# An SSM and MLP gradient kernel: ten staging rows and moved parameter turns in the front, four seed columns and four doublings in the Y tables

## Chip, cores and metric

The kernel runs on one core of one Trainium2 chip. The metric is the device time of one execution in microseconds (us). The core has a matrix engine (PE, TensorE), a vector engine (DVE, VectorE), a scalar engine (ACT, ScalarE), a general engine (POOL, GpSimd) and a queue engine (SP, SyncE). DMAs are issued on the queues of SP, ACT and POOL.

## What is computed

The reference mixes two branches by a gate and returns the result and all gradients of it. In its core (dt, A, B, C are the state model's parameters for 448 channels with 256 complex states each, L = 2048 positions; the MLP's hidden width is 1792):

```python
g = sigmoid((u * gate_w).sum(-1))
P = exp(dt * A * l)                             # 448 x 256 x 2048
K = einsum("dn,dnl,dn->dl", C, P, dt * B).real  # 448 x 2048
a = irfft(rfft(pad(u)) * rfft(pad(K)))[:L] + u * Dskip
h = relu(u @ w1 + b1) ** 2
out = g * a + (1 - g) * (h @ w2 + b2)
# and the gradients of out (weighted with grad_out) in u, A, B, C, log_dt, Dskip, w1, b1, w2, b2, gate_w
```

## The kernel before

The work falls into a front, a loop over 14 chunks of states and a tail. The order of the instructions on each engine is made by a scheduler when the kernel is built; a statement may be placed behind another one with `tc.issue_after`. All transfers of SP and ACT go over a few shared semaphores, and an issue waits until the transfer before it on its semaphore has landed.

**The front** (about 0 to 236 us). u and grad_out are loaded in eight and four pieces on SP's and ACT's queues (L401, L411). `fwd1` (L219 to L241) is the first stage of the forward Fourier transform. It goes over eight blocks; a block makes four products (L229), evacuates them from PSUM into one staging row (L206, L207, L216) of 128 x 4 x 448, and stores its two halves to a tensor in memory, `gd`: the first half on POOL's queue, the second on SP's (L238). It runs on u first, with four rows in the buffer F17; the first five blocks are evacuated by ACT alone, the others by ACT and DVE in turn. On SP's queue the six parameters A, B, C (real, imaginary) are turned by DMA transposes (L420 to L423), and the constants M2, MI, Etw and sel are loaded (L424 to L426). These ten issues stand ahead of the second-half stores. The gate is computed (L456 to L463), DA = grad_out * g (L465), and `fwd1` runs on DA with six rows in R32 (L494). Then follow the parameter mathematics on DVE, with an exponential and a sine on ACT (L526 to L551), and `transposed` (L471 to L486), which turns u on PE, copies each block out of PSUM with ACT and DVE in turn (L483) into a ring of three slots, and spills a slot to memory on POOL's queue (L485). A second call does the same for DB = grad_out * (1 - g).

`powers(gr)` (L617 to L647) makes the records of a group of four chunks (two in the last group): starting from the transition factor of each state it squares ten times (ACT's Square L643, DVE L644 and L645), and ACT copies each power into the record (L640). A record has 1920 columns: four X seeds, the X powers, two Y seed columns (a one, set by POOL at L615, and one power) and five Y powers. The record of a group is stored on ACT's queue (L647). Groups alternate between a record buffer in F17 and one in R32. Between the groups run the spectra (`spectrum`, L657) and the first inverse transforms (`inv1p`, L280) of the products; their results are loaded back, summed (L713) and stored (dk).

**The chunk loop** (L965 to L1006, about 184 to 625 us). For each chunk DVE builds an X table (L794, L773 to L777) and a Y table: `build_y` copies the seed columns (L825) and doubles the table five times; each doubling (`double`) is three DVE instructions (L784, L785, L787), the last doubling in two halves. `expand_y` on ACT (L812, L814) widens the powers for the doublings, one chunk ahead. PE multiplies the tables into the convolution kernel (L844), turns them (L870, L882) and makes the chunk's gradient (L913 on PE, L917 on ACT, L933 on DVE, L942 on PE). Between these the scheduler places the MLP's products on PE: the hidden layer (L584, L587), the output (L1021), turns of the weights (L1045, L1056) and the first gradient products (L1084, L1087, with ACT L1089 and DVE L1096).

**The tail** (from about 651 us). The convolution kernel is loaded, the transform `fwd1` runs on it (L229 with the tensor `gd` number 2), and it stands in PE's order behind all of the output products L1021. The output, the weight gradients (L1158 to L1195), the parameter gradients and the last stores follow.

## Time and profile before

| | |
|---|---|
| median of 7 runs | 943.05 us (934.66 to 947.1) |
| the profiled execution | 944.72 us |
| its span in the profile | 942.5 us |
| its granted TensorE clock, mean | 0.833 of full speed |
| PE, DVE, ACT, POOL busy | 705.3, 670.9, 579.3, 191.8 us |
| u landed | 13.70 us |
| seed copies of the 14 chunks (L794) begin | 184.16, 214.30, 259.20, 291.22, 318.98, 346.68, 374.44, 402.17, 429.91, 460.02, 490.66, 526.87, 559.64, 591.48 us |
| bytes moved by DMA | 184.96 MB |

The profile is of one execution; its time is 2.2 us longer than the span, which runs from the first to the last instruction that the profiler shows. Busy time of an engine leaves out its waits and its DMA issues. A line such as "L216" is a line of the kernel's source; where a helper holds the instruction, several places of the kernel share the line, and the tile's name tells them apart (F is the buffer F17, R is R32, S is S25). In the lists of waits the name behind the arrow is what came last before the engine went on. A chain of waits follows what ended last back to what released it.

### The profile page before, as it was taken

The page shows a single profiled execution, that of the slowest core. Times are in us where ns is not written, and L with a number is a line of the kernel's source. Part 1 is how long each engine was busy: PE and PEld are TensorE (multiplying, and loading weights), DVE is VectorE, ACT ScalarE, POOL GpSimd, SP SyncE. Part 2 cuts the span into 40 slices and gives each one's busy share as a digit, 9 for nine tenths or more (in the row PEclk, how much of TensorE's full clock was granted, in tenths as well). Part 3 has the DMA queues.
Part 4 walks back from the last instruction along what each step waited for, and adds up shares of the span by engine and source line. Part 5 has one row for each costly group of instructions (what it writes and reads, how often), then busy time and mean ns, then how long its engine had stood idle before and what let it go on. Part 6 is the DMA issues. An engine that isn't in the chain of part 4 may idle for free.

```text
span 942.5 us, 18829 instructions
## 1 busy us (share of the span) xinstructions
PE 705.3 (75%) x7553; PEld 337.1 (36%) x7585; DVE 670.9 (71%) x1152; ACT 579.3 (61%) x927; POOL 191.8 (20%) x327
## 2 busy tenths in 40 slices
PE   3345675636878898788987898789958888959896
PEld 1122222214344443334443443444323334524343
DVE  4387985787389999999886899864219954159820
ACT  3346757725997879778686766564526644536543
POOL 2141000113202122121202311223201021343221
PEclk9686565668869999989966997999979778978799
DMA  9986486797536766446742964659997997589862
GB/s 188 254 254 242 161 308 254 277 319 232 119 82 126 156 137 121 117 102 144 179 104 77 246 160 125 124 144 282 331 377 241 245 281 234 180 211 288 205 149 73
DMA packets 170814, 184.96 MB, mean 196 GB/s; under 512 B 100467, under 2 KB 146968, under 8 KB 169800
## 3 DMA queue, kind: packets, MB, share of 16 engines
q1 hardware_dynamic: 121462, 84.74, 37.7%
q0 software_dynamic: 19904, 59.15, 19.6%
q10 hardware_dynamic: 29362, 39.88, 13.0%
q8 instruction: 59, 0.97, 0.4%
q14 instruction: 27, 0.22, 0.1%
HBM read 88.22 MB, written 73.13 MB: 171 GB/s over the span
## 4 chain that ended last, share of the span: by engine, by line
DVE 31%; DMA 18%; PE 18%; issue 14%; ACT 12%; POOL 4%; SPq 2%; ACTq 1%; POOLq 0%; DVEq 0%
DVE P L933 4%; DVE F L785 4%; PE psF L1169 3%; PE psN L1021 3%; DMA S<-rT_d 3%; DVE K L787 2%; DVE K L784 2%; DVE X L773 2%; DVE Y L787 2%; SPq L422 2%; DVE F L774 2%; DVE Y L784 2%; DMA hd<-st 2%; DVE X L777 1%; DMA D<-hd 1%
## 5 line engine op out<-in xcount | busy, mean ns | idle before, releaser
L933 DVE TENSOR_TENSOR P<-R 128x2048 bf16<-128x2048 bf16 x42 | 49.5, 1218 | 23.9 <-ACT R L917 21.1
L1169 PEld LDWEIGHTS <-S 128*128 128x128 bf16 x448 | 43.6, 104 | 59.9 <-issue 15.1
L917 ACT CAST R<-psF 128x1024 bf16<-128x1024 f32 x56 | 57.4, 1024 | 11.8 <-PE psF L913 11.7
L1021 PE MATMUL psN<-D,S 128*128 128x448 bf16 x208 | 52.5, 385 | 4.8 <-ACT S L591 4.8
L1169 PE MATMUL psF<-U,S 128*128 128x448 bf16 x224 | 51.7, 381 | 2.1 <-ACT S L1164 2.0
L913 PE MATMUL psF<-R,S 64*32 64x256 bf16 (+1 forms) x1344 | 37.9, 295 | 9.7 <-DMA R<-Y 5.2
L584 PE MATMUL psN<-S,U 128*128 128x512 bf16 x119 | 37.3, 419 | 10.2 <-ACT F L589 4.9
L1084 PE MATMUL psN<-S,U 128*128 128x512 bf16 x113 | 37.1, 441 | 7.5 <-ACT D L1089 5.5
L207 DVE CAST K<-psN 128x448 bf16<-128x448 f32 x36 | 21.6, 619 | 27.1 <-PE psN L255 26.9
L773 DVE TENSOR_TENSOR X<-X,F 128x512 bf16<-128x512 bf16 (+1 forms) x70 | 37.4, 535 | 4.6 <-ACT F L807 2.6
L784 DVE TENSOR_TENSOR K<-K,F 128x2048 bf16<-128x2048 bf16 (+3 forms) x42 | 36.4, 866 | 4.5 <-ACT F L812 2.9
L1097 POOL DMA_DIRECT2D dhT_d<-D x28 | 20.2, 721 | 90.9 <-DVE D L1096 90.7
L785 DVE TENSOR_TENSOR F<-K,F 128x2048 bf16<-128x2048 bf16 (+3 forms) x42 | 35.9, 855 | 3.1 <-ACT F L814 3.1
L784 DVE TENSOR_TENSOR Y<-Y,F 128x2048 bf16<-128x2048 bf16 (+3 forms) x42 | 36.3, 864 | 1.6
L774 DVE TENSOR_TENSOR F<-X,F 128x512 bf16<-128x512 bf16 (+1 forms) x70 | 36.9, 528 | 0.6
L787 DVE TENSOR_TENSOR K<-K,F 128x2048 bf16<-128x2048 bf16 (+3 forms) x42 | 36.3, 865 | 1.3
L787 DVE TENSOR_TENSOR Y<-Y,F 128x2048 bf16<-128x2048 bf16 (+3 forms) x42 | 36.3, 864 | 1.3
L1364 DVE SCALAR_TENSOR_TENSOR F<-psN,Y 128x448 bf16<-128x448 f32 x16 | 9.9, 616 | 36.9 <-PE psN L329 36.9
L785 DVE TENSOR_TENSOR F<-Y,F 128x2048 bf16<-128x2048 bf16 (+3 forms) x42 | 35.9, 854 | 0.3 <-ACT F L814 0.3
L1021 PE MATMUL psN<-S,D 128*128 128x448 bf16 x168 | 35.7, 361 | 0.0
L883 ACT COPY M<-psX 128x1024 bf16<-128x1024 bf16 x26 | 26.6, 1022 | 14.1 <-PE psX L882 14.1
L913 PEld LDWEIGHTS <-S 64*16 64x16 bf16 (+1 forms) x1792 | 22.4, 90 | 33.4 <-issue 28.5
(385 smaller groups left out, 1930.0 us busy)
## 6 DMA issues: line engine op xcount, KB each, us to landing
sp<-K ACTq DMA_DIRECT2D x8, 896.0 KB, 4.8
hd<-st ACTq DMA_DIRECT2D x16, 448.0 KB, 4.4
dhT_d<-D POOLq DMA_DIRECT2D x28, 256.0 KB, 5.3
R<-sp SPq DMA_DIRECT2D x8, 896.0 KB, 21.4
S<-rT_d POOLq DMA_DIRECT2D x14, 512.0 KB, 5.2
R<-hd SPq DMA_DIRECT2D x16, 448.0 KB, 7.2
rec_d<-F ACTq DMA_DIRECT2D x2, 1920.0 KB, 9.1
Y<-gd SPq DMA_DIRECT2D x4, 896.0 KB, 5.1
```

The lines of the kernel that those rows point to most:

```text
L584: T_.matmul(ps[:], lhsT=w1w[:, dt, j * P:j * P + P], rhs=ub[:, dt], start=(dt == 0), stop=False, skip_group_check=True)
L773: V.tensor_tensor(out=hi4, in0=lo, in1=bcast_dims(pr, [0, (None, n), 1]), op=ALU.mult)
L774: V.tensor_tensor(out=Vv.rearrange("p (x a r) -> p x a r", x=2 * W2, r=2), in0=lo, in1=bcast_dims(pi, [0, (None, n), 1]), op=ALU.mult)
L784: V.tensor_tensor(out=hi, in0=lo, in1=bcast_dims(pr, [0, (None, n // 2), 1]), op=ALU.mult)
L785: V.tensor_tensor(out=Vv.rearrange("p (x a q) -> p x a q", x=rows, q=2), in0=lo, in1=bcast_dims(pi, [0, (None, n // 2), 1]), op=ALU.mult)
L787: return V.tensor_tensor(out=T4[:, :, :, n:2 * n], in0=T4[:, :, :, n:2 * n], in1=V4, op=ALU.add)
L913: T_.matmul(psz[32 * ii:32 * ii + m, t, 256 * s:256 * s + 256], lhsT=DKc[64 * t:64 * t + 64, s, g, 2 * ii:2 * ii + 1 + par].rearrange("p i ...
L917: S.copy(zb[:, :, :, gg].rearrange("p s t n -> p t s n"), psz[:].rearrange("p t (s n) -> p t s n", s=2))
L933: lastp = V.tensor_tensor(out=pr.rearrange("p s t g n -> p s t (g n)"), in0=zv, in1=(xb if r == 0 else rev_dim(xb, 2)), op=ALU.mult)
L1021: lastm = T_.matmul(ps[:, 0:D], lhsT=hblk[j][:, P * tt:P * tt + P], rhs=ws[:, j, :], start=(w == 1 and j == 0), stop=(j == FT - 1))
L1084: T_.matmul(ps[:], lhsT=w2Tw[:, jp, dt, j % 2], rhs=dblk[:, dt], start=(dt == 0), stop=False, skip_group_check=True)
L1169: lastm = T_.matmul(ps[:, 0:width], lhsT=hh[:, t, :], rhs=(DB2[:, t, :] if w == 0 else U[:, t, 0:D + 1]), start=(t == 0), stop=(t == LT - 1))
```

## The change

- **Staging rows.** Both calls of `fwd1` take their rows from one list of ten (four in F17, six in R32). u takes F0 to F3 and R0 to R3, DA goes on with R4, R5, F0 to F3, R0, R1. DA's second-half stores are issued on ACT's queue.
- **Turns and constants.** The six parameter turns stay on SP's queue and are placed behind u's last second-half store. M2, MI, Etw and sel are loaded from ACT's queue; in the order of the built program they stand ahead of ACT's first evacuation.
- **transposed(u).** All eight copies are ACT's. The call for DB alternates as before.
- **Records.** A record has 2048 columns: four Y seed columns and four Y powers. The columns are one, the powers after two and after three squarings, and their product, which POOL makes with six tensor_tensor instructions a group (four products into a scratch behind DB in D16, a difference and a sum). The store of the record is issued on POOL's queue. Scratch buffers of the odd groups lie elsewhere.
- **Y tables.** The seed copy has four columns a row (128x512), and four doublings follow instead of five: the smallest, whose DVE instructions were 128x256, is gone. `expand_y` widens four levels (L812 on 128x1024, L814 on 128x512). A chunk's Y record load is 256 KB, not 224.
- **Tail.** A small row moves into the tile of the last Y record; the other line there is cut to the width in use.

```diff
 GC = 2
 W2 = 2 * CC
 NLEV = 11
-RS = 1920
+RS = 2048
 NA = 16
 AOFF = [0, 1, 2, 3, 256, 258, 512, 768, 1024, 1280, 1536, 1792, 2048]
 VA = len(AOFF)
...
         self.st_i = 0
         self.st_more = []
         self.q2 = tc.nc.gpsimd
+        self.q3 = tc.nc.sync
         self.pair_i = 0
         self.pairs3 = True
         self.act_only = False
...
                 j0base = 32 * hh + q * 4
                 for g2 in range(2):
                     dst = bass.AP(tensor=gd, offset=(j0base + 16 * g2) * 64 * D, ap=[[D, 64], [64 * D, 4], [1, D]])
-                    d = (self.q2 if g2 == 0 else nc.sync).dma_start(dst, st[g2 * 64:(g2 + 1) * 64])
+                    d = (self.q2 if g2 == 0 else self.q3).dma_start(dst, st[g2 * 64:(g2 + 1) * 64])
                     if g2 == 0:
                         last = d
+                    else:
+                        self.last_st = d
         return last
 
     def load_s1(self, gd, q, s1, queue=None):
...
         nonlocal o
         o += n
         return prm[:, o - n:o]
-    for nm, src in (("Ar", A_A_re), ("Ai", A_A_im), ("Br", A_B_re), ("Bi", A_B_im), ("Cr", A_C_re), ("Ci", A_C_im)):
-        r = carve(2 * D).rearrange("p (h d) -> p h d", h=2)
-        nc.sync.dma_start_transpose(out=r, in_=src)
-        raw[nm] = r
-    load_const("M2", nc.sync)
+    load_const("M2", nc.scalar)
     for nm in ("MI", "Etw", "sel"):
-        load_const(nm, nc.sync)
+        load_const(nm, nc.scalar)
     K.M2, K.MI, K.Et = ct["M2"], ct["MI"], ct["Etw"]
     sel = ct["sel"][:].rearrange("p (k m) -> p k m", k=4)
-    DB = K.t("D16", [P, LT, D])
+    DBt = K.t("D16", [P, 8192])
+    DB = DBt[:, 0:LT * D].rearrange("p (t d) -> p t d", d=D)
     ident = const.tile([P, P], bf16, name="ident")
     make_identity(nc, ident[:])
     brow_np = np.array([4.0 * (i % 64) for i in range(128)], np.float32).reshape(128, 1)
...
     K.F1 = ct["F1BD"]
     RA = K.t("R32", [P, 16384])
     Fs = K.t("F17", [P, 8704])
-    stage = [[b[:, 1792 * i:1792 * i + 1792].rearrange("p (a d) -> p a d", d=D) for i in range(k)] for b, k in ((Fs, 4), (RA, 6))]
-    K.fwd1(lambda j: U[:, j, 0:D], gd[0], stage[0], 5)
-    u_ev, u_dv, u_f1 = K.last_ev, K.last_dv, K.last_f1
+    stage = [b[:, 1792 * i:1792 * i + 1792].rearrange("p (a d) -> p a d", d=D) for b, k in ((Fs, 4), (RA, 6)) for i in range(k)]
+    K.fwd1(lambda j: U[:, j, 0:D], gd[0], stage, 5)
+    u_ev, u_dv, u_f1, u_st = K.last_ev, K.last_dv, K.last_f1, K.last_st
+    with tc.issue_after(u_st.ins):
+        for nm, src in (("Ar", A_A_re), ("Ai", A_A_im), ("Br", A_B_re), ("Bi", A_B_im), ("Cr", A_C_re), ("Ci", A_C_im)):
+            r = carve(2 * D).rearrange("p (h d) -> p h d", h=2)
+            nc.sync.dma_start_transpose(out=r, in_=src)
+            raw[nm] = r
     s32 = const.tile([P, LT], fp32, name="s32")
     s_b = const.tile([P, LT], bf16, name="s_b")
     g_b = const.tile([P, LT], bf16, name="g_b")
...
     SB = K.t("S25", [P, 12800])
     turn = SB[:, 4096:12288].rearrange("p (k a l) -> p k a l", k=4, a=DT)
 
-    def transposed(src, spill):
+    def transposed(src, spill, cps):
         nonlocal nti
         for t2 in range(LT // 2):
             ps = K.ps(NT[4 + nti % 2], [P, DT, 2 * P], bf16)
...
                     sv = src[:, 2 * t2 + tt, dt * P:dt * P + DSZ[dt]]
                     for h in range(1 if dt < 3 else 2):
                         T_.transpose(ps[64 * h:64 * h + DSZ[dt], dt, tt * P:tt * P + P], sv, ident[:], tile_position=(0, 64 * h))
-            cp = S.copy if t2 % 2 == 0 else V.tensor_copy
+            cp = cps[t2 % 2]
             lb, k = t2 // 2, t2 % 2
             cp(turn[:, lb % 3, :, 256 * k:256 * k + 256], ps[:])
             if k == 1:
...
     V.tensor_copy(b1_f[:], ps[:])
     ld4 = b1_f[:, FT:FT + 4]
 
-    lf1 = K.fwd1(lambda j: DA[:, j, :], gd[1], stage[1])
+    K.q3 = nc.scalar
+    lf1 = K.fwd1(lambda j: DA[:, j, :], gd[1], stage)
+    K.q3 = nc.sync
     SX, SY = prm, K.t("Y16", [P, 8192])
     s1r = [b[:, 3584 * i:3584 * i + 3584].rearrange("p (a d) -> p a d", d=D) for b in (SY, SX) for i in range(2)]
 
...
     for q in range(2):
         l11 = s1_load(1, q)
     with tc.issue_after(u_f1.ins):
-        transposed(U, UT_d)
+        transposed(U, UT_d, (S.copy, S.copy))
     for t in range(LT):
         V.tensor_scalar(out=DB[:, t, :], in0=G[:, t, :], scalar1=omg32[:, t:t + 1], scalar2=None, op0=ALU.mult)
     ps = K.ps("S", [P, 512])
...
 
 
     Fp = K.t("F17", [P, 8704])
-    psets = [(Fp[:, 0:4 * RS], RA[:, 14336:16384], W0[:, 3584:4608]), (RA[:, 0:4 * RS], RA[:, 7680:9728], RA[:, 9728:10752])]
+    psets = [(Fp[:, 0:4 * RS], RA[:, 14336:16384], W0[:, 3584:4608]), (RA[:, 0:4 * RS], RA[:, 8192:10240], SY[:, 7168:8192])]
 
     def fields(r):
 
         xs = r[:, :, 0:512].rearrange("p c (t w e) -> p c t w e", t=2, e=4)
-        ys = r[:, :, 1024:1280].rearrange("p c (w t e) -> p c t w e", t=2, e=2)
+        ys = r[:, :, 1024:1536].rearrange("p c (w t e) -> p c t w e", t=2, e=4)
         lx = r[:, :, 512:1024].rearrange("p c (t l w) -> p c t w l", t=2, w=W2)
-        ly = r[:, :, 1280:1920].rearrange("p c (t l w) -> p c t w l", t=2, w=W2)
+        ly = r[:, :, 1536:2048].rearrange("p c (t l w) -> p c t w l", t=2, w=W2)
         return xs, ys, lx, ly
     for rb, _, _ in psets:
         xs, ys, _, _ = fields(rb.rearrange("p (c r) -> p c r", c=4))
...
         V.tensor_tensor(out=xs[:, :, 1, :, 3], in0=ua[:, :, 1], in1=va[:, :, 0], op=ALU.add)
         x, y = lam, halves(cur[0])
         for k in range(NLEV):
-            dst = xs[..., 2] if k == 0 else ys[..., 1] if k == 2 else lx[..., (1, 8, 9, 10).index(k)] if k in (1, 8, 9, 10) else ly[..., k - 3]
+            dst = xs[..., 2] if k == 0 else ys[..., k - 1] if k in (2, 3) else lx[..., (1, 8, 9, 10).index(k)] if k in (1, 8, 9, 10) else ly[..., k - 4]
             S.copy(dst.rearrange("p c t w -> p t c w"), x)
             if k < NLEV - 1:
                 sq = halves(sqr)
...
                 V.scalar_tensor_tensor(out=y[:, 1], in0=x[:, 0], scalar=2.0, in1=x[:, 1], op0=ALU.mult, op1=ALU.mult)
                 V.tensor_tensor(out=y[:, 0], in0=sq[:, 0], in1=sq[:, 1], op=ALU.subtract)
                 x, y = y, halves(cur[1 - k % 2])
-        nc.scalar.dma_start(bass.AP(tensor=rec_d, offset=4 * gr * P * RS, ap=[[RS, P], [P * RS, nch], [1, RS]]), R)
+        vs = [DBt[:, 7168 + 512 * i:7168 + 128 * nch + 512 * i].rearrange("p (c t w) -> p c t w", t=2, w=W2) for i in range(2)]
+        for i in range(2):
+            for t in range(2):
+                G_.tensor_tensor(out=vs[i][:, :, t], in0=ys[:, :, t, :, 1], in1=ys[:, :, i, :, 2], op=ALU.mult)
+        G_.tensor_tensor(out=ys[:, :, 0, :, 3], in0=vs[0][:, :, 0], in1=vs[1][:, :, 1], op=ALU.subtract)
+        G_.tensor_tensor(out=ys[:, :, 1, :, 3], in0=vs[0][:, :, 1], in1=vs[1][:, :, 0], op=ALU.add)
+        G_.dma_start(bass.AP(tensor=rec_d, offset=4 * gr * P * RS, ap=[[RS, P], [P * RS, nch], [1, RS]]), R)
 
 
     spw = K.t("K28", [P, 4, 4, 2, D])
...
             K.inv1p(pr, 2 * q + h, hd[0])
         if q == 0:
             with tc.issue_after(f10.ins):
-                transposed(DB, DBT_d)
+                transposed(DB, DBT_d, (S.copy, V.tensor_copy))
         if q < 2:
             powers(q + 2)
     with tc.issue_after(ls1.ins):
-        nc.sync.dma_start(bass.AP(tensor=DB_d, offset=0, ap=[[LT * D, P], [1, LT * D]]), flat(DB))
+        nc.sync.dma_start(bass.AP(tensor=DB_d, offset=0, ap=[[LT * D, P], [1, LT * D]]), DBt[:, 0:LT * D])
         load_const("Ew", nc.sync)
         NW2 = 32 * len(ekeys) - 4096
         Ew2 = SB[:, 10752:10752 + NW2]
...
         load_ut(1)
     Fv = K.t("F17", [P, 8704])
     Vt = Fv[:, 0:4096]
-    PRY = Fv[:, 4096:5376].rearrange("p (l w t d) -> p l w t d", l=5, t=2, d=2)
-    PIY = Fv[:, 5376:6656].rearrange("p (l w t d) -> p l w t d", l=5, t=2, d=2)
+    PRY = Fv[:, 4096:5120].rearrange("p (l w t d) -> p l w t d", l=4, t=2, d=2)
+    PIY = Fv[:, 5120:6144].rearrange("p (l w t d) -> p l w t d", l=4, t=2, d=2)
     PRX = Fv[:, 6656:7680].rearrange("p (l t w d) -> p l t w d", l=4, t=2, d=2)
     PIX = Fv[:, 7680:8704].rearrange("p (l t w d) -> p l t w d", l=4, t=2, d=2)
     DKs = SB[:, 10752:12800].rearrange("p (k s g i a) -> p k s g i a", k=2, s=2, g=NG, a=NA)
...
         (G_ if c == 1 else nc.sync).dma_start(rx_[c][:], bass.AP(tensor=rec_d, offset=c * P * RS, ap=[[RS, P], [1, 1024]]))
 
     def load_ry(c):
-        ry_[c] = K.t("recy", [P, 896])
-        return (G_ if c == 1 else nc.sync).dma_start(ry_[c][:], bass.AP(tensor=rec_d, offset=c * P * RS + 1024, ap=[[RS, P], [1, 896]]))
+        ry_[c] = K.t("recy", [P, 1024])
+        return (G_ if c == 1 else nc.sync).dma_start(ry_[c][:], bass.AP(tensor=rec_d, offset=c * P * RS + 1024, ap=[[RS, P], [1, 1024]]))
 
     def expand_x(c):
         lr, li = (rx_[c][:, 512 + 256 * k:768 + 256 * k].rearrange("p (l w) -> p l w", w=W2).unsqueeze(3).to_broadcast([P, 4, W2, 2]) for k in range(2))
...
             S.mul(PRX[:, :, t], lr, 1.0)
             S.mul(PIX[:, :, t], li, 1.0 - 2.0 * t)
 
-    def expand_y(c, l0=0, l1=5):
+    def expand_y(c, l0=0, l1=4):
         n, a, b = W2 * (l1 - l0), W2 * l0, W2 * l1
-        S.mul(PRY.rearrange("p l w t d -> p (l w) (t d)")[:, a:b], ry_[c][:, 256 + a:256 + b].unsqueeze(2).to_broadcast([P, n, 4]), 1.0)
+        S.mul(PRY.rearrange("p l w t d -> p (l w) (t d)")[:, a:b], ry_[c][:, 512 + a:512 + b].unsqueeze(2).to_broadcast([P, n, 4]), 1.0)
         for t in range(2):
-            S.mul(PIY.rearrange("p l w t d -> p (l w) t d")[:, a:b, t], ry_[c][:, 576 + a:576 + b].unsqueeze(2).to_broadcast([P, n, 2]), 1.0 - 2.0 * t)
+            S.mul(PIY.rearrange("p l w t d -> p (l w) t d")[:, a:b, t], ry_[c][:, 768 + a:768 + b].unsqueeze(2).to_broadcast([P, n, 2]), 1.0 - 2.0 * t)
 
     def build_x(c):
         for (s0, st, dst, n, k) in ((0, 1, 2, 2, 0), (0, 2, 4, 2, 1), (0, 4, 6, 2, 2), (0, 4, 8, 2, 3), (6, 1, 10, 3, 3)):
...
         Y4 = Ys[c % 2]
         with tc.issue_after(after.ins):
             if half == 0:
-                V.tensor_copy(Y4.rearrange("p w t b -> p (w t) b")[:, :, 0:2], ry_[c][:, 0:256].rearrange("p (x e) -> p x e", e=2))
-            for k in (range(5) if half == 0 else (4,)):
-                ws = slice(0, W2) if k < 4 else slice(CC * half, CC * half + CC)
+                V.tensor_copy(Y4.rearrange("p w t b -> p (w t) b")[:, :, 0:4], ry_[c][:, 0:512].rearrange("p (x e) -> p x e", e=4))
+            for k in (range(4) if half == 0 else (3,)):
+                ws = slice(0, W2) if k < 3 else slice(CC * half, CC * half + CC)
                 rows = 2 * (ws.stop - ws.start)
-                last = double(Y4[:, ws].rearrange("p w t b -> p (w t) b"), 2 << k, Y4[:, ws], PRY[:, k, ws].rearrange("p w t d -> p (w t) d"),
+                last = double(Y4[:, ws].rearrange("p w t b -> p (w t) b"), 4 << k, Y4[:, ws], PRY[:, k, ws].rearrange("p w t d -> p (w t) d"),
                               PIY[:, k, ws].rearrange("p w t d -> p (w t) d"), rows=rows)
         return last
 
...
                         lry1 = lry if c == 0 else lry1
                         expand_x(c + 1)
                         if c == 0:
-                            expand_y(1, 0, 4)
+                            expand_y(1, 0, 3)
                     elif c == 0:
-                        expand_y(1, 4, 5)
+                        expand_y(1, 3, 4)
                     else:
                         expand_y(c + 1)
                 if half == 0:
...
```

More of the change, by code (lines that the diff above doesn't have):

```diff
@@ L1338 @@
     S.mul(negI[:], ident[:], -1.0)
-    rcx, rcy = K.t("recx", [P, 1024]), K.t("recy", [P, 896])
+    rcx, rcy = K.t("recx", [P, 1024]), K.t("recy", [P, 1024])
     dgt = rcx[:, 0:256].rearrange("p (k m) -> p k m", k=2)
-    row = rcy[0:1].rearrange("p (k d) -> p k d", k=2)
+    row = rcy[0:1, 0:2 * D].rearrange("p (k d) -> p k d", k=2)
     dg = const.tile([P, LT], fp32, name="dg")
@@ L1406 @@
     T_.transpose(ps[0:4], dlog_b[:], ident[:])
-    drow = const.tile([4, P], bf16, name="drow")
-    S.copy(drow[:], ps[0:4])
+    drow = rcy[0:4, 2 * D:1024]
+    S.copy(drow, ps[0:4])
     G_.dma_start(out_8[0:384].rearrange("(t p) -> t p", p=P), drow[0:3])
```

## The prediction, made before the changed kernel ran

> **What bounds the kernel now.** I read the chain of waits for the first 90 us first, since half of the change stands there. Its columns are start, length and what held the chain.
>
> ```profile
> 2.13 11.55 DMA U<-in_A_u_dram
> 13.70 1.33 SPq L422
> 15.08 4.67 SPq L422
> 19.80 5.41 SPq L422
> ...
> 33.98 4.37 DMA gd<-F
> 38.45 0.91 ACT F L216
> ...
> 51.86 6.78 DMA gd<-R
> ...
> 72.22 8.14 DMA UT_d<-S
> 80.38 1.01 ACT S L483
> 81.41 1.28 ACT L546
> ```
>
> u lands at 13.70. Then six parameter turns hold SP's queue for 1.33+4.67+5.41+1.29+1.76+1.77 = 16.2 us, four constants follow, and only at 33.98 goes the store of u's last staging row, which sets the fifth row free at 38.45. Later a store of transposed u (72.22 to 80.38) holds a copy on ACT, and behind that copy stands the sine's table load (81.41). The list of waits puts prices on it (total us, times, longest):
>
> ```profile
> DVE F L207 <- DMA gd<-F: 15.3, 1, 15.3
> ACT F L216 <- DMA gd<-F: 14.6, 1, 14.6
> ...
> ACT S L483 <- DMA UT_d<-S: 6.6, 1, 6.6
> ```
>
> So both evacuating engines stand still for 15 us. The busy times by stretch say how much of that can come back, and what bounds the rest: columns are busy us of PE, PE's weight load, DVE, ACT and POOL with instruction counts, PE clock, DMA share, GB/s.
>
> ```profile
> 24.00:47.00 23.00, 7.56 (x38) 3.36 (x37) 6.77 (x22) 7.26 (x13) 2.54 (x4) 0.63 1.01 258
> ...
> 94.00:141.00 47.00, 31.67 (x152) 11.95 (x152) 42.59 (x91) 29.70 (x52) 0.00 (x0) 0.60 0.62 234
> 141.00:190.00 49.00, 28.86 (x148) 11.21 (x147) 31.91 (x72) 37.61 (x73) 5.97 (x7) 0.62 0.70 270
> ...
> 262.00:430.00 168.00, 140.13 (x2270) 70.45 (x2265) 163.50 (x235) 139.27 (x193) 31.76 (x53) 0.90 0.56 121
> 430.00:500.00 70.00, 58.93 (x1011) 34.26 (x1011) 62.88 (x99) 52.71 (x70) 12.03 (x22) 0.79 0.58 133
> ...
> 625.00:655.00 30.00, 26.20 (x308) 13.25 (x306) 10.36 (x14) 14.98 (x24) 11.23 (x20) 0.94 0.90 237
> ```
>
> In the stall the DMA engines are full (1.01), so the stall is partly a queue for bandwidth. From 94 to 190 DVE leads, then ACT. From 262 to 430, six chunks, DVE is busy 163.5 of 168 us: a chunk takes 27.75 us (from one seed copy, L794, to the next) and is DVE-bound. After 430 chunks take 30 to 36 us, with PE at 81 to 84% and DVE at 77 to 93%: no engine alone bounds them. Over 236 to 655 PE works 21.7+140.1+58.9+36.5+67.3+26.2 = 351 of 419 us; the 68 us of idle are all that this stretch can give while PE's work is the same.
>
> [...]
>
> **Part 1, the front.** With ten rows u's eight staging rows never wait, so 15 us of stall go; the turns stand behind u's stores. What takes the place: on ACT's queue four constants (about 1.4 MB) now stand ahead of ACT's first evacuation, and in the program's waits each stands behind a u or G load on the same DMA semaphore. I put u's first evacuation at about 21 us, not 13 (estimate: u lands from 13.7 on, G after it). u then takes some 12 us (before: 10 us to 23.8 while u was still landing, 5.5 us after 38.45), to 33; DA begins at about 37, not 44. The turns take their 16 us on SP from about 33 and land at about 55; DA's second stores, now on ACT's queue, wait for semaphores that turns hold, and stop ACT's evacuations behind them. Before, DA's evacuation ended at 60 and DVE's parameter work began at 59.98. All DMA bytes up to there are the same, and that stretch is full (2 to 66 us at 0.9 to 1.0), so I take 57: 3 us gained. Bounds: 8 gained (DA from 37 without a check, its own 16 us: 53, after that the turns) and 6 lost (last turn lands late).
>
> The 8.14 us store: in the new order of ACT the first copies of u stand far earlier, so the ring's slot is free in time, and the sine, whose input was done at 75.89, loses its 81.41-75.89 = 5.5 us. Against it all eight copies of u go to ACT: four more at 1.01 us; DVE is rid of four at 0.69 us, 2.7 us. ACT idles 9.5 us for DVE (L539 for L537) in this stretch, so I count a third of the 4 us: 5.5-1.4 = 4 us gained (0 to 6). Front: -7 us (range -14 to +6). All up to 236 us hangs on it, in sequence.
>
> **Part 2, the records.** Twenty-four GpSimd instructions, six a group, 256 elements each (128 in the last group)[...]. The column needs powers 1 and 2 of ys; between power 3 and the last power 18 us pass (ACT L640, 101.7 to 119.4 in the first group), so the store of the record waits for none of it, and POOL does nothing from 94 to 141. That is the cover[...]. The store moves from ACT's to POOL's queue: POOL issues take 0.5 to 0.75 us, and 2048 columns for 1920 are 7% on a 9.09 us transfer, +0.6 us, for which DVE waited 0.9 and 4.67 us. The unknown is the lock. [...] I take +3 (0 to 14). A gain is excluded: no engine is relieved but ACT's queue.
>
> **Part 3, the chunk loop.** Each chunk loses the two small doublings' three instructions once: the rows 128x256 of L784, L785, L787 are 0.40, 0.37 and 0.40 us, 1.18 us; the seed copy doubles but L794's copy of that size takes 0.286 against 0.279. 14 x 1.18 = 16.5 us off DVE. ACT loses 0.22 us at L812 (1.27 to 1.05) and twice 0.11 at L814 (0.73 to 0.63): 0.43 a chunk, 6 us. In the six DVE-bound chunks 7 us are gained at once.
>
> What is late next: PE. The scheduler fills PE by DVE's pace, and the new instruction order has fewer MLP products between chunks (L584 42 to 35-37 a pair, L1084 57-59 to 42) and more behind the last: L1084 52 to 84, L1087 18 to 28, L1021 112 to 117. That is 32 x 0.441 + 10 x 0.433 + 5 x 0.37 = 20.3 us, at the 87% PE reached from 625 to 655: 23 us more behind the loop. The products of gd2 (L229, at 651 before) stand behind all of it. The loop must therefore end 23 us earlier to be even. Sources: 7 us in the six bound chunks, 9.5 us DVE in the other eight, and fewer products in those that PE delayed. If the eight later chunks fall from 32.3 us on average to 28, some 26+7 = 33: gain 10. If they lose their DVE share only: 16.5-23 = 6.5 lost. I take PE's idle down by 4 of 68: -4 us (range -10 to +7).
>
> **Part 4, the tail.** From L229 on the orders are alike; 655 to 700 is full of DMA (share 1.01, 369 GB/s). 0 (-2 to +2).
>
> **Sum:** -7+3-4+0 = -8 us from the profiled execution, 944.72 (span 942.5 and 2.2 around it): 936.7. That execution lies 1.7 us above the median 943.05 of the runs, so 935.
>
> **The rivals.** (a) Both gains come in full: later chunks fall to 28 us, the front gives 10, the lock 1: -10-10+1 = -19, so 924. For it: PE idles 16% in the later chunks, in waits that a shorter DVE turn removes; against it: the PE order there is fixed, and waits on ACT (L1084 <- L1089, 5.5 us) remain. (b) The stall only changes its name: DMA is full to 66 us, constants and turns cost the same bytes, parameter work begins at 60 as before, the ring's 4 us pay for the lock's 3, and the loop gives nothing: -1, so 942. For it: the share 1.01; against it: 15 us idle on both engines. (c) Slower: the filler behind the loop. One mechanism: products moved behind the chunks cost 23 us there, while the loop shortens by DVE's 16.5 us only, some of it where ACT or PE is last (then about 7+4 = 11): +12; with front -7 and lock +3 that is +8, so 951. It decides once the loop shortens by less than 23-4 = 19 us. For it: DVE is busy 97% from 262 to 430, so fewer products buy nothing there; against it: PE and DVE alternate as the last ones after 430.
>
> **How the numbers follow.** Forecast 935 (its own range 929 to 941) 0.45; (a) 0.2; (b) 0.13; (c) 0.22. The range 922 to 951 takes in the cases and leaves out the ends of the front's and the lock's bounds. A measurement of this kernel tells about 0.5%, 4.7 us: faster is below 938.3, slower above 947.8. From the forecast some 0.38 and from (a) 0.2 are faster, with a little of (b): 0.6; (c) less a part that stays within, and a late turn: 0.22; between: 0.18.
>
> **What would show it.** In the profile after: no wait of ACT L216 or DVE L207 for gd<-F, but one on ACT's queue at the constants; DVE's first parameter work (L529) at 57; the sine's table load before 79; [...]L645 or L278 with longer means if the lock bites; chunks between 262 and 430 at 26.6 us; L229 of gd2 at 651 less 8. The prediction is wrong if parameter work begins after 62, if DVE's means at 94 to 190 grow by over 10%, or if PE idles over 72 us between its first hidden product and gd2.

## The result, and the profile after

The changed kernel takes 949.98 us (median of 24 runs) against 942.78 us of the kernel before (61 runs). The ratio is 1.0086, with a 95% interval of 1.0065 to 1.0107: slower by about 0.9%, where 935 was forecast. Medians here and below are over all executions, the ratios leave out those more than 1.5% above the fastest one of their kernel, and five of the profiles below (of the seed columns in the X seeds' order, of the new records with the old front, of the loop alone, and of the last two rows of the last table) are of such slower executions. The profiled execution has a span of 948.2 us at a mean clock of 0.833, so it compares directly with the 942.5 us at 0.833 of before. Line numbers of the changed kernel are higher by up to 13: L216 is L217 there, L640 is L647, L645 is L652, L933 is L946, L942 is L955, L1084 is L1097.

Dated by the same instructions, the two profiles divide like this (us):

| stretch | before | after | difference | forecast |
|---|---|---|---|---|
| start to the first copy of a power (L640) | 88.5 | 88.0 | -0.5 | -7 |
| from there to the last power copied | 98.5 | 112.7 | +14.2 | +3 |
| last power to the first hidden product | 32.1 | 32.3 | +0.2 | |
| first hidden product to the end of the last L942 | 428.0 | 408.5 | -19.5 | |
| from there to the first product of gd2 (L229) | 3.9 | 16.5 | +12.6 | |
| the two above together: the loop | 431.9 | 425.0 | -6.9 | -4 |
| gd2 to the end | 291.5 | 290.2 | -1.3 | 0 |

The loss stands in one row, the making of the powers, and the missing gain in the first.

The list of waits for the first 90 us of the changed kernel (total us, times, longest) answers to the one of before:

```profile
ACT L207 <- DMA M<-c_M: 24.4, 1, 24.4
...
PE psN L258 <- DMA Y<-gd: 11.6, 1, 11.6
...
ACT R L207 <- DVE R L217: 9.2, 1, 9.2
...
ACT F L217 <- issue: 7.6, 1, 7.6
...
DVE R L540 <- DMA X<-in_A_C_im_dram: 4.7, 1, 4.7
```

The 15 us waits for gd<-F are gone. In their place ACT begins at 24.4 (the name M shows the constants at the head of its queue) with a table load of 1.28 us, and its first evacuation is at 25.70. It stands 7.6 us in the middle of DA's evacuations while its queue holds a store back, and DVE waits 4.7 us for the last turn, which lands at 60.05. PE stands 11.6 us in front of DA's last three products: in this build the second stage of u's transform (L258), for which gd is loaded back (Y<-gd, issued at 56.24 on SP's queue, behind the last turn), comes ahead of them; before, it came behind them. The 9.2 us of ACT end with the evacuation of these products, so DA is evacuated at 68.8, not at 60.

One more wait stands in DVE's timeline (start, length), before and then after, with a row of POOL's from the same time:

```profile
71.83 1.07 DVE L558 TENSOR_SCALAR D<-K,omg 128x448 bf16<-128x448 bf16 x4
```

```profile
74.89 3.19 DVE L565 TENSOR_SCALAR D<-K,omg 128x448 bf16<-128x448 bf16 x4
75.78 1.44 POOL L622 MEMSET R<- 128x256 bf16 x1
```

The first of the four instructions takes 2.46 us instead of 0.33 and ends 0.13 us after this memset, POOL's last one. POOL's memsets set the records' first columns to one and zero. One into the four Y seed columns takes 1.4 us, into the two of before it took 0.8, and they now come at the same time as this work of DVE.

The busy times by stretch, columns as before:

```profile
24.00:47.00 23.00, 17.45 (x79) 6.97 (x78) 10.35 (x28) 20.43 (x36) 7.44 (x11) 0.87 0.82 229
...
94.00:141.00 47.00, 28.99 (x134) 11.66 (x135) 35.73 (x66) 31.96 (x45) 12.05 (x14) 0.54 0.51 190
141.00:190.00 49.00, 26.29 (x106) 8.82 (x106) 33.32 (x68) 35.17 (x55) 10.62 (x15) 0.50 0.59 228
...
262.00:430.00 168.00, 137.45 (x2289) 69.70 (x2298) 150.44 (x212) 136.81 (x193) 31.08 (x52) 0.88 0.58 125
430.00:500.00 70.00, 58.99 (x859) 29.35 (x848) 65.72 (x86) 56.63 (x79) 12.45 (x21) 0.90 0.66 137
...
625.00:655.00 30.00, 27.81 (x274) 12.78 (x271) 9.67 (x12) 17.06 (x27) 13.35 (x22) 1.00 0.84 242
```

From 94 to 141 DVE falls from 42.59 to 35.73 busy us and gets through 66 instructions instead of 91: something else is last. From 262 to 430 it falls from 163.5 to 150.4 busy us, but the six chunks there take 174.0 us instead of 170.7: DVE no longer bounds them.

What is last from 94 on shows in ACT's timeline (start, length). Before:

```profile
93.51 0.62 ACT L640 CAST F<-R 128x512 bf16<-128x512 f32 x1 [1.09 <-DVE R L645]
...
96.26 1.34 ACT L640 CAST F<-R 128x512 bf16<-128x512 f32 x1 [0.75 <-DVE R L645]
...
101.72 0.62 ACT L640 CAST F<-R 128x512 bf16<-128x512 f32 x1 [2.85 <-DVE R L645]
```

and after:

```profile
93.82 2.48 ACT L647 CAST F<-R 128x512 bf16<-128x512 f32 x1
95.80 0.92 ACT L650 ACTIVATE P<-R 128x512 f32<-128x512 f32 x1
...
97.53 2.48 ACT L647 CAST F<-R 128x512 bf16<-128x512 f32 x1
```

The rows of before are the powers 1, 2 and 3: 0.62 us into adjacent columns, 1.34 into the Y seeds of two columns (a step of 8 bytes), 0.62 again. After, the powers 2 and 3 both go into seeds of four columns, where the next element of a row lies 16 bytes on: 2.48 us each, and no idle time stands before them. The square that makes the next power follows the copy on ACT, so 1.14 + 1.86 = 3.0 us a full group lie in the chain of squarings, and the square behind takes 0.92 instead of 0.63 to 0.68.

GpSimd's part, first its own rows, then DVE's at the same time:

```profile
100.10 2.93 POOL L657 TENSOR_TENSOR D<-F 128x256 bf16<-128x256 bf16 x4 [16.21 <-ACT F L647]
102.99 1.51 POOL L659 TENSOR_TENSOR F<-D 128x256 bf16<-128x256 bf16 x1
104.11 1.53 POOL L658 TENSOR_TENSOR F<-D 128x256 bf16<-128x256 bf16 x1
```

```profile
101.71 0.81 DVE L652 TENSOR_TENSOR R<-P 128x256 f32<-128x256 f32 x1
102.45 0.86 DVE L651 SCALAR_TENSOR_TENSOR R<-P 128x256 f32<-128x256 f32 x1
103.24 1.04 DVE L651 SCALAR_TENSOR_TENSOR R<-R 128x256 f32<-128x256 f32 x1
...
106.07 0.41 DVE L652 TENSOR_TENSOR R<-P 128x256 f32<-128x256 f32 x1
```

DVE's two-input instructions of 0.41 us take 0.8 to 1.0 while GpSimd works and 0.41 just after it. POOL's queue issues the first group's store only behind the second group's six instructions, at 125.22; the group's last power is done at 123.07. DVE, which needs the buffer again, waits for it (before, the waits for these stores were 0.9 and 4.7 us):

```profile
DVE F L642 <- DMA rec_d<-F: 6.5, 1, 6.5
```

### The profile page after: what moved, and what is told of

Its sections match the earlier page's. It is cut to its first block, busy times and chain, and to the rows that moved or that the text cites. A ratio compares the mean times of both kernels' runs of the same rounds, so it can differ in the third digit from the quotient of the medians.

```text
span 948.2 us, 18816 instructions
## 1 busy us (share of the span) xinstructions
PE 706.0 (74%) x7553; PEld 334.6 (35%) x7585; DVE 662.8 (70%) x1106; ACT 588.0 (62%) x931; POOL 216.0 (23%) x355
## 3 DMA queue, kind: packets, MB, share of 16 engines
q10 hardware_dynamic: 30258, 36.26, 12.6%
## 5 line engine op out<-in xcount | busy, mean ns | idle before, releaser
L946 DVE TENSOR_TENSOR P<-R 128x2048 bf16<-128x2048 bf16 x42 | 49.5, 1219 | 27.5 <-ACT R L930 25.9
L1182 PE MATMUL psF<-U,S 128*128 128x448 bf16 x224 | 49.1, 367 | 2.4 <-ACT S L1177 2.4
L926 PE MATMUL psF<-R,S 64*32 64x256 bf16 (+1 forms) x1344 | 35.4, 281 | 17.3 <-DMA R<-K 5.1
L786 DVE TENSOR_TENSOR X<-X,F 128x512 bf16<-128x512 bf16 (+1 forms) x70 | 37.5, 535 | 6.1 <-ACT F L820 4.2
L258 PEld LDWEIGHTS <-M 128*64 128x64 bf16 x192 | 14.3, 134 | 72.3 <-issue 68.7
L1097 PE MATMUL psN<-S,U 128*128 128x512 bf16 x114 | 34.4, 404 | 4.0 <-ACT D L1102 2.9
L797 DVE TENSOR_TENSOR Y<-Y,F 128x2048 bf16<-128x2048 bf16 (+2 forms) x35 | 33.5, 958 | 1.4
L797 DVE TENSOR_TENSOR K<-K,F 128x2048 bf16<-128x2048 bf16 (+2 forms) x35 | 33.5, 957 | 1.3
L800 DVE TENSOR_TENSOR K<-K,F 128x2048 bf16<-128x2048 bf16 (+2 forms) x35 | 33.5, 958 | 1.1
L800 DVE TENSOR_TENSOR Y<-Y,F 128x2048 bf16<-128x2048 bf16 (+2 forms) x35 | 33.5, 958 | 1.1
L790 DVE TENSOR_TENSOR X<-X,F 128x512 bf16<-128x512 bf16 (+1 forms) x70 | 32.3, 462 | 1.8
## 6 DMA issues: line engine op xcount, KB each, us to landing
R<-sp SPq DMA_DIRECT2D x8, 896.0 KB, 13.9
```

Of the source, the lines that this page charges most:

```text
L786: V.tensor_tensor(out=hi4, in0=lo, in1=bcast_dims(pr, [0, (None, n), 1]), op=ALU.mult)
L790: return V.tensor_tensor(out=hit, in0=hit, in1=V4, op=ALU.add)
L797: V.tensor_tensor(out=hi, in0=lo, in1=bcast_dims(pr, [0, (None, n // 2), 1]), op=ALU.mult)
L800: return V.tensor_tensor(out=T4[:, :, :, n:2 * n], in0=T4[:, :, :, n:2 * n], in1=V4, op=ALU.add)
L926: T_.matmul(psz[32 * ii:32 * ii + m, t, 256 * s:256 * s + 256], lhsT=DKc[64 * t:64 * t + 64, s, g, 2 * ii:2 * ii + 1 + par].rearrange("p i ...
L946: lastp = V.tensor_tensor(out=pr.rearrange("p s t g n -> p s t (g n)"), in0=zv, in1=(xb if r == 0 else rev_dim(xb, 2)), op=ALU.mult)
```

## The experiments

Theory at the start: (S) the write step of ACT's two copies, (L) GpSimd's exclusion of DVE, as the expectations call the longer DVE instructions beside GpSimd's (0.41 us to 0.8 and more above; the forecast says lock), and (Q) the record's store, queued on POOL behind the next group's GpSimd work, make the records dear; (F) the new front yields nothing; (P) the loop gives back part of its gain to products behind it. Rivals: the front is the loss; the exclusion is all of the loss; the filler behind the loop (rival c of the prediction) is the loss. Each run is compared with runs of the kernel before on the same chip.

**The seed columns in the X seeds' order.**

```diff
-ys = r[:, :, 1024:1536].rearrange("p c (w t e) -> p c t w e", t=2, e=4)
+ys = r[:, :, 1024:1536].rearrange("p c (t w e) -> p c t w e", t=2, e=4)
```

(the seed copy of the loop reads accordingly)

> The changed kernel with the record's four Y seed columns laid out as the X ones are (t, w, e): ACT's two copies of a power into them write at a step of 8 bytes instead of 16; the seed copy reads the other order. The order of the loop's products on PE stays as in the changed kernel. Theory (the write step of ACT's copies is the main cost of the new records: 2.48 us a copy in the squaring chain, where 1.34 and 0.62 stood): the copies fall to 1.33 us, two in a group, 3.5 groups, 8 us, so the last power is done at about 192 instead of 200.7 and the kernel takes about 942. Rival (GpSimd's exclusion of DVE is the main cost): the last power moves by at most 2 us, about 949.

944.13 us, ratio 1.0024 (0.9999 to 1.0050). The last power is done at 194.3, 6.4 us sooner, where 8 were expected. S, the write step, holds, and the rival that GpSimd is all of it falls; about half of what the powers had lost (13.7 us at the last one) is left.

**The two fronts.** The new records with the old front, and the old records with the new front (the diff of the change, its front part alone undone or done).

> The new records and four doublings with the front of the kernel before (four and six staging rows, turns and constants ahead of the stores on SP, transposed u copied by ACT and DVE in turn). Theory (the new front neither gains nor loses: its stall on u's rows is replaced by waits of ACT for constants and for store slots): powers begin at about 88 and the kernel takes 949 plus or minus 2, as with the new front. Rival one (the prediction's: the new front gains some 7): 956. Rival two (the new front is what costs): about 943.

> The new front alone, with the records and the five doublings of the kernel before. Theory (the front yields nothing): powers begin at 88 as before, 943 plus or minus 2. Rival one (the prediction's): 936. Rival two (the front costs, and the records are free): 950.

The new front alone: 940.77 us, ratio 0.9979 (0.9950 to 1.0007), powers from 85.0 us. The new records with the old front: 960.15, ratio 1.0185 (1.0120 to 1.0251), last power at 203.1 instead of 200.7. So the front is not the loss. F, that it yields nothing, is too hard on it with the new records, where it is worth about 1% (the old front's run has six executions only); with the old records its interval reaches to no change at all. In the profile of this second run PE stands 13.0 us for nothing that the profile shows, so its later stretches are not used; a cleaner comparison follows below.

**The record's store back on ACT's queue.**

```diff
-        G_.dma_start(bass.AP(tensor=rec_d, offset=4 * gr * P * RS, ap=[[RS, P], [P * RS, nch], [1, RS]]), R)
+        nc.scalar.dma_start(bass.AP(tensor=rec_d, offset=4 * gr * P * RS, ap=[[RS, P], [P * RS, nch], [1, RS]]), R)
```

> The changed kernel with the record's store back on ACT's queue. The build's order then also keeps more MLP products between the chunks: L1097 66 behind the last chunk instead of 84. Theory (on POOL's queue the store of group 0 stands behind the six GpSimd instructions of group 1, and DVE waits 6.5 us at group 2 for its landing): the store goes out some 5 us sooner, that wait falls below 2 us, the last power is done at about 195, and with 18 products fewer behind the loop, about 941. Rival (the store's queue doesn't matter; copies and lock do): last power at 200, 948.

A miss: 954.57 us, ratio 1.0127 (1.0068 to 1.0186), six executions. DVE's wait for the store of group 0 is gone (6.5 to 0 us), but one of 4.2 us comes at the next group, and the last power is done at 201.3. So Q, the store's place, is not a cost that goes away by this move. That the whole is slower is not settled: the tail from gd2 took 298.2 us, at a clock of 0.85 against 0.88, and PE waited 3.7 us for transposed DB.

**The fourth column left out.** (The six GpSimd instructions are taken away, and the column is set once.)

> The changed kernel without GpSimd's six instructions a group: the fourth Y seed column is not computed (it is set once to one and zero, so the Y tables are not the reference's); order of the loop as in the changed kernel. Theory (GpSimd's part costs by shutting DVE out, some 2 to 2.7 us a group, and by standing ahead of the record's store on POOL's queue): L651, L652 and L281 fall back to 0.42 and 0.62 us, the store of group 0 goes out at about 117 instead of 125, the last power is done at about 192 instead of 200.7, about 942. Rival (the copies' write step is all of it): last power at 199, 948.

947.59 us, ratio 1.0042 (1.0011 to 1.0073). From the first to the last power it is 104.5 us instead of 112.7, so the GpSimd part is worth 8.2 us there. The groups of DVE by shape (busy us, mean ns, then idle before), first before the change, then after, then of this run:

```profile
L278 DVE TENSOR_TENSOR U<-K 128x896 bf16<-128x896 bf16 x24 | 14.0, 618 | 0.2 <-ACT K L216 0.2
...
L645 DVE TENSOR_TENSOR R<-P 128x256 f32<-128x256 f32 x20 | 8.4, 421 | 6.0 <-ACT P L643 6.0
```

```profile
L281 DVE TENSOR_TENSOR U<-K 128x896 bf16<-128x896 bf16 x24 | 15.9, 694 | 0.0
...
L652 DVE TENSOR_TENSOR R<-P 128x256 f32<-128x256 f32 x20 | 9.9, 497 | 5.3 <-ACT P L650 5.3
```

```profile
L281 DVE TENSOR_TENSOR U<-K 128x896 bf16<-128x896 bf16 x24 | 14.0, 618 | 0.2 <-ACT K L217 0.2
...
L653 DVE TENSOR_TENSOR R<-P 128x256 f32<-128x256 f32 x20 | 8.4, 420 | 5.3 <-ACT P L651 5.3
```

The means of 694 and 497 ns go back to those of before. From the first to the last power DVE is busy 88.5 us instead of 95.6 for the same work (sum of its instructions), so L, the exclusion, can account for most of the 8.2 us. The wait for the store of group 0 is gone here too. In this execution the powers began 3.3 us later than after, which is why the last one, at 195.8, misses the 192 expected: the memsets that this run adds on POOL hold the same instruction of L565 for 7.1 us. The time lies between theory and rival.

**The columns in stretches of their own, and with the product on DVE.**

```diff
-"p c (w t e) -> p c t w e"
+"p c (e t w) -> p c t w e"
...
-            for t in range(2):
-                G_.tensor_tensor(out=vs[i][:, :, t], in0=ys[:, :, t, :, 1], in1=ys[:, :, i, :, 2], op=ALU.mult)
+            V.tensor_tensor(out=vs[i], in0=ys[:, :, :, :, 1], in1=ys[:, :, i, :, 2].unsqueeze(2).to_broadcast([P, nch, 2, W2]), op=ALU.mult)
```

(the second part in the second run alone, where the difference and the sum go to DVE too; the seed copy of the loop reads accordingly in both)

> The changed kernel with each of the four Y seed columns in a stretch of its own (e, t, w), so that ACT's copies write without a step; the seed copy in the loop reads with a step instead. Theory (write step): L647 at 0.62 us for both powers, against 2.48 with a step of 16 bytes and 1.33 with 8: 3.5 groups by 2 by 1.86 = 13 us less on ACT's part of the chain; last power at 188 to 190, 940. The seed copy may lose up to 0.3 us a chunk. Rival (after the step of 8 bytes, which gave 6.4 us, other work of the chain is last): last power at 194, 944.

> As the run with the columns in stretches of their own, and the fourth column made by four DVE instructions a group instead of six of GpSimd. In this build the products between the chunks are nearly those of the kernel before. Theory (write step, exclusion and the store's place were the costs of the new records): four DVE instructions at about 0.4 us a group, 5 us in all, but no exclusion and the store's wait gone: last power at 188, about 937. Rival (the record's work can't be had for less than the loop gains): 943.

946.30 us, ratio 1.0025 (0.9998 to 1.0052), and 933.61 us, ratio 0.9840 (0.9769 to 0.9911, six executions). In the first, L647 takes 0.62 us for both powers:

```profile
L647 ACT CAST F<-R x20: 601/618/628, 88.0 to 169.5; 128x512 bf16<-128x512 f32 x20
```

The last one is done at 186.8, even sooner than expected; 4.2 of the 13.9 us come from an earlier begin, 83.8 instead of 88.0. But the time isn't better than with the step of 8 bytes: from the first hidden product to gd2 it takes 433.4 us, after 425.0. The seed copy in the loop gathers from four stretches now, and in the second run, then in the run with both repairs further below, its line is:

```profile
L837 DVE COPY Y<-recy x7: 1293/1301/1315, 190.1 to 553.9; 128x512 bf16<-128x512 bf16 x7
```

```profile
L837 DVE COPY Y<-recy x7: 273/282/291, 192.5 to 550.9; 128x512 bf16<-128x512 bf16 x7
```

That is 1.3 us instead of 0.28 to 0.30 a chunk, 14 us in all. The 0.3 us a chunk that I had allowed were wrong. Yet the second run is as fast as the run with both repairs, which lacks those 14 us: its stretch from the first hidden product to gd2 is 422.0 us, that run's 421.9. It has 58 products of L1084 behind the last chunk, the other 84. So DVE time in the loop seems to have been exchanged for products behind it at no net cost; no run changed one without the other.

**The loop alone**, on the kernel before.

```diff
-[:, :, 0:2], ry_[c][:, 0:256].rearrange("p (x e) -> p x e", e=2))
-            for k in (range(5) if half == 0 else (4,)):
+[:, :, 0:4].rearrange("p x (f e) -> p x f e", e=2), ry_[c][:, 0:256].rearrange("p (x e) -> p x e", e=2).unsqueeze(2).to_broadcast([P, 2 * W2, 2, 2]))
+            for k in (range(1, 5) if half == 0 else (4,)):
```

> The kernel before (its front, its records, its ACT work) with four doublings: the seed copy writes each of the two stored columns twice and the smallest doubling is left out, so the Y tables are not the reference's. This is the loop's part of the change alone, 16.5 us off DVE. In the build's order 28 products of L1084 and 10 of L1087 more stand behind the last chunk (17 us). Theory (part of the gain is given back by these products and by DVE waiting for PE): 4 us faster, 938. Rival one (DVE bounds the loop and all comes through): 928. Rival two (the products behind the loop cost more than DVE's gain): 946.

939.20 us, ratio 0.9882 (0.9803 to 0.9961), six executions. The loop's part is a gain of 0.4 to 2%. That excludes the mechanism of rival (c), filler dearer than the gain; it excludes neither the full 16.5 us nor the 4 us.

**One repair, both repairs, and two fronts with both.** Product on DVE alone; product on DVE and the step of 8 bytes; these two and the constants behind the turns on SP's queue; both repairs with the old front.

```diff
-    load_const("M2", nc.scalar)
-    for nm in ("MI", "Etw", "sel"):
-        load_const(nm, nc.scalar)
...
             nc.sync.dma_start_transpose(out=r, in_=src)
             raw[nm] = r
+        for nm in ("M2", "MI", "Etw", "sel"):
+            load_const(nm, nc.sync)
```

> The changed kernel with the one change that the fourth column is made by four DVE instructions a group instead of six of GpSimd; ACT's copies keep their write step of 16 bytes. Theory (GpSimd's part, its exclusion of DVE and the store behind it, is worth about 8 us up to the last power, and DVE's own part costs 1.5 us a group): last power at 194, about 943. Rival (the work costs the same on either engine): last power at 200, 949.

> The changed kernel with both repairs of the records: seed columns in (t, w, e), a write step of 8 bytes, and the fourth column by four DVE instructions a group instead of six of GpSimd. The loop's order is that of the changed kernel (84 products of L1097 behind the last chunk). Theory (write step and GpSimd's exclusion made the records dear; the loop itself gains some 7 net): ACT's copies at 1.33 us, DVE's and the store's waits gone, last power at 184 to 188 instead of 200.7, seed copy in the loop at 0.29 us; 934. Rival (the low time of the run with stretches and DVE product came from its order of the products, 58 behind the last chunk): 943.

> As the run with both repairs, and the four constants loaded on SP's queue behind the parameter turns instead of on ACT's ahead of its first evacuation. Theory (ACT's 24.4 us of waiting at the start is what ate the front's gain): u's first evacuation at 13 to 15 instead of 24.4, parameter work begins at 50 or earlier, powers begin some 5 us sooner, 929. Rival (the DMA engines and the turns set the pace; an earlier evacuation only waits elsewhere): powers begin within 2 us of the other run, 934.

> As the run with both repairs, with the front of the kernel before. Theory (the new front is worth 0 to 3 us): 1 to 3 us slower than with the new front, 936. Rival (with the new records the new front is worth 10 us, as the first comparison of fronts with new records suggested): 944.

| run | median us | ratio to before | last power |
|---|---|---|---|
| the change as made | 949.98 | 1.0086 (1.0065 to 1.0107) | 200.7 |
| product on DVE | 944.11 | 1.0022 (0.9997 to 1.0047) | 194.8 |
| and step of 8 bytes | 932.90 | 0.9894 (0.9860 to 0.9928) | 181.7 |
| and constants behind the turns | 928.39 (six executions) | 0.9849 (0.9796 to 0.9902) | 174.3 |
| both repairs, old front | 938.31 | 0.9949 (0.9922 to 0.9976) | 189.5 |

All four came within 3 us of the theory's time, but the difference of the two fronts was 5 us where 1 to 3 were expected. In the run with both repairs ACT's timeline has the two copies at 1.33 us, and a wait for DVE before the second again:

```profile
92.99 1.33 ACT L647 CAST F<-R 128x512 bf16<-128x512 f32 x1
...
96.08 1.35 ACT L647 CAST F<-R 128x512 bf16<-128x512 f32 x1 [0.48 <-DVE R L652]
```

With the constants moved, the waits of the first 70 us show ACT beginning on u's landing, no longer on the constants:

```profile
ACT L207 <- DMA U<-in_A_u_dram: 11.4, 1, 11.4
```

The parameter work begins at 42.9 instead of 54.9 there and the powers at 78.0 instead of 86.7. With and without the new front, both repaired: 0.9894 against 0.9949, so the new front is worth some 0.5%, 5 us, though the two intervals just touch. Its constants on ACT's queue held the powers back by 8.7 us in these profiles; by the ratios that is another 0.45%, but those intervals overlap, so the gain in time is not settled. The rival that the fast run owed its time to its order of products falls, since the run with both repairs has the order of the change.

## Why the prediction was wrong

**Part 2 is the step that failed.** "So the store of the record waits for none of it" and "no engine is relieved but ACT's queue" cost the records by GpSimd's instructions and the store alone. The widening of the seeds from two columns to four also changes where ACT's copies write, and I gave these two copies a group no term at all. The price was in the profile of before: copies of one size at 0.62 us into adjacent columns and at 1.34 us into columns 8 bytes apart. At 16 bytes it took another doubling, 2.48 us, in a chain where ACT and DVE take turns. Going to 8 bytes took 6.4 us off the last power with GpSimd in place and 13.1 us (194.8 to 181.7) with the product on DVE; by the ratios the step is worth 1.3%, 12 us, in the second case. The other term, the exclusion, I had at +3 with 14 as its upper bound. Both were estimates that no number of the profile of before carries: POOL was idle there from 94 to 141. Measured, leaving GpSimd's part out took 8.2 us off the way to the last power (ratio 1.0086 to 1.0042), moving it to DVE took 4.6 us off (1.0086 to 1.0022, 0.6%). The trace of after shows it in the lengths alone: the two-input instructions of 0.41 us took up to 1.04 beside GpSimd's, and L645's and L278's means rose from 421 and 618 to 497 and 694 ns. The six instructions took 5.5 us in the first group, of which four took 0.73 each and two, writing with the step of 16 bytes, 1.5. The store did wait, behind the next group's six instructions (issued at 125.22, the group's last power done at 123.07), and DVE 6.5 us for the store. "A gain is excluded" was wrong too: with both repairs the stretch from first to last power takes 95.0 us, 3.5 less than before, and DVE's waits of 0.9 and 4.7 us for the records' stores are gone. That the store's new queue makes this gain is likely, but no run shows it alone.

**Part 1** had its moves right and its sum wrong in this pair of profiles: DA at 37.9 (37 forecast), parameter work at 52.8 (57 forecast), no wait for gd<-F, none of transposed u for its ring. What I mis-sized is what stands between: u's first evacuation at 25.7, not 21; the last turn at 60.05, not 55. What I left out is the new order on PE, which puts DA's last products behind gd's way to memory and back (11.6 us). The parameter work began 7 us sooner than before and stood for the last turn (4.7 us) and for those products (3.6 us), so the exponential came at 74.11, 3.7 us later than before. Beside POOL's memsets DVE then took another 2 us (2.46 for 0.33), and the sine's input was done at 80.65 instead of 75.89. So what the ring no longer costs was used up: the sine's load is at 79.46 instead of 81.41, and powers began at 88.0 against 88.5. By the ratios the front is worth 0.2% with the old records (not clear of noise) and 0.5% with the repaired ones: 2 to 5 us against the 7 forecast.

**Part 3** was right in sign, and its parts moved as described. The first term failed: the six chunks that were DVE-bound gained nothing of the 7 us. Their seed copies begin at 269.71, 305.31, 333.56, 361.34, 388.00 and 417.06 us, the next chunk's at 443.65: one takes 35.6 us and the others 26.6 to 29.1. DVE now waits there for PE (list of waits, 270 to 444 us):

```profile
DVE P L946 <- PE psN L955: 7.2, 4, 2.4
```

In the run of the loop alone the same six take 166.8 us instead of 170.7, and four of them 26.6 to 26.8 as forecast. So the shorter DVE turn can come through, and what keeps it back after the change, the order of the products or something else, is open. The gain came later: the next five chunks took 151.1 us instead of 161.6. (The forecast's "eight later chunks" are six; its 26 us are right for six.) The products behind the loop cost 12.6 us, not 23. That cost follows their number over the builds: with 52 products of L1084 behind the last chunk's L844 the gap from L942 to gd2 is 3.9 us (before, and the new front alone), with 58 it is 6.4, with 66 11.2, with 75 13.3, with 80 15.1, with 84 16.5 to 16.7. This is a relation across builds that differ in other things too; no run changed the number alone. The loop's net is -6.9 us in the profiles, and 0.4 to 2% (4 to 19 us) in the times of the run of the loop alone, against the 4 forecast.

**Part 4** held: 291.5 and 290.2 us.

Of the rivals, (c) was on the right side by its time, 951, for another reason: the loop shortened by 19.5 us, more than its threshold of 19, and only the 12.6 us came behind it.

## What to carry to other kernels

When an edit widens an interleaved layout, cost every instruction that writes into it, not only those the edit adds (here ACT's copies, and POOL's memsets as well, 0.8 to 1.4 us): look for the same operation at two steps in the profile before (here 0.62 us into adjacent columns, 1.34 at 8 bytes), and don't take the wider step at the old price (16 bytes took 2.48). In this chain, where two engines take turns, most of what one of them was relieved of counted (8 us off ACT's copies, worked out from 2.48 and 1.33, moved the last power by 6.4), and the idle third engine was no free one, since DVE's instructions of 0.41 us took up to 1.04 beside it. This loop, with DVE at 97% (163.5 of 168 us), gained nothing there from a DVE load 8% smaller (150.4 us), and DVE waited 7.2 us for PE; take the gain from the whole loop, not from its busiest stretch.

## What was not expected of the hardware

- ACT's copy of 128x512 from 32 to 16 bits: 0.62 us into adjacent columns, 1.33 at a step of 8 bytes, 2.48 at 16; the Square right behind a copy of the last kind took 0.92 instead of 0.63.
- DVE's copy of 128x512 in 16 bits took 0.29 us reading runs of four and 1.30 us gathering from four stretches.
- DVE's multiply of 128x448 in 16 bits with one tensor input, 0.33 us alone, took longer beside POOL's memsets, which read nothing. In each run where it began among them, it ended within 0.25 us after the last of them: it took 2.46 us after the change (memsets with a step of 16 bytes, 1.4 us each), 1.31 with both repairs (8 bytes, 0.8 us) and 0.56 with the columns in stretches of their own (no step, 0.4 us).
- Four DVE instructions a group in place of six of GpSimd made the kernel 0.6% faster, though before the change POOL was idle from 94 to 141 us and DVE busy 91% of it.
